# One fused recurrence and feed-forward kernel: the first group made of one chunk from each batch, in 64-token halves, with a third load buffer and a new opening order

## The chip, the cores and the metric

The kernel runs on one core of one Trainium2 chip. The metric is device microseconds for one execution, lower is better. Before the change the median is 487.1 us over three executions (487.08 to 487.21).

## What is computed

Two stages. The first is a linear recurrence over 768 time steps for 4 batches of 8 heads with head size 48. The state of a head is a 48x48 matrix that decays per row and step. The second is a feed-forward layer over all 3,072 tokens, from 384 to 2,048 and back, with x·sigmoid(1.702x) between.

```python
def _attn_ref(r, k, v, w, u):            # (4, 8, 768, 48)
    for t in range(S):
        cur = einsum('bhd,bhe->bhde', u[None] * kt, vt)
        y[:, :, t] = einsum('bhd,bhde->bhe', rt, state + cur)
        state = wt[:, :, :, None] * state + einsum('bhd,bhe->bhde', kt, vt)

def _moe_ref(x, w_in, w_out):            # x (3072, 384), w_in (384, 2048), w_out (2048, 384)
    h = x @ w_in
    return (h * (1.0 / (1.0 + exp(-1.702 * h)))) @ w_out
```

## The kernel before

The recurrence is cut into 24 chunks of 128 tokens, six for each batch. A chunk is one generator, `chunk(t)`, whose pieces are the tokens `a<t>` in the order. Its work by engine is this. VectorE runs two scans of the decays (`L419` backward, `L425` forward), the product `rku` (`L432`), and the decayed keys and queries `kq` (`L440`, `L441`). TensorE makes the bonus of a token with itself (`ps_d`, `L448`), the transposed keys (`ps_t`, `L474`), the sum of keys and values that carries the state on (`ps_u`, `L505`) and the scores of token pairs (`ps_e` or `ps_s`, `L523`). ScalarE fills the diagonal of the score matrix `am` with the bonus, one head at a time (`L494`), VectorE copies the scores behind the diagonal into it (`copy_predicated`, `L574`), and TensorE multiplies the state and the values with queries and `am` into `ps_y` (`L530`, `L617`). Chunks are numbered along time within a batch, so chunk `t` needs the state that chunk `t-1` left, save at the four batch starts 0, 6, 12 and 18. On VectorE that state costs a scaling (`L459`) and an addition (`L511`) in each chunk.

From chunk 6 on (`HALF`) the scores are made for two halves of 64 tokens (`token_halves`). The matrices are 64 wide there and four of them share the array; the state is carried to the middle of the chunk (`mid`) and on. There the scores of chunk `t+1` and the output of chunk `t` are issued as one run of matmuls (`one_run`, `L293`). A chunk in `ALONE` is not joined to the one ahead of it.

The output of a chunk becomes a column block of `x`, held as a high part (`hi`, float32r) and a rest (`lo`). In the first group, `ps_y` is copied to `hi` by ScalarE (`L631`), a matmul with a negative identity takes `hi` off `ps_y` (`L635`), and ScalarE copies what is left to `lo` (`L636`). `x` uses 112 rows for three blocks of heads; rows of the fourth are moved into the 16 free rows at each end by six small transfers `x<-x` (`fill_x`, `L645`, token `x2`), three on the SP queue and three on POOL's. The fourth chunk of the first group is written into its place at once.

Four chunks make a group of 512 tokens, and a group has 16 tasks, one per 128 of the 2,048 hidden features. A task is a first product (`g`, nine matmuls `ph<-x,pair`), the gelu (`h`), and a second product (`y`, nine matmuls into three accumulators `po`). There are 96 tasks. The first 20 run as 128-row matmuls (`L677`, `L707` to `L709`); the rest as pairs on two 64-row halves (`rows_of`, `L733`).

Weights are split into pairs of high and low parts on the chip. `f<i>` fetches the raw weights in 1 MB pieces, even `i` from `w_in`, odd from `w_out`; `w<i>` converts them: two passes on ScalarE (`L222`, `L223`), two on VectorE (`L225`, `L228`), a cast on ScalarE (`L231`) and a difference on VectorE (`L233`).

Until task 20 the order of all this is written out by hand in `RAMP`: a token is one piece of a generator. `l<t>` is a piece of the load of a chunk: the decays with keys and receptances (`wkr_t`), and the values (`v_t`). `k<n>` issues `n` filler matmuls (`idle<-d1r`) with no use of their result. After task 20 the order follows from `rest()`. Loads of decays, keys and receptances land in two buffers (`lands`), so the load of chunk 2 is issued when chunk 0 is done with its own. Chunks below `CROSS` are loaded in one to three transfers, later ones in nine, with the head pairs swapped.

## Time and profile before

| | |
|---|---|
| median of three executions | 487.1 us |
| the profiled execution | 486.55 us |
| its span on the core | 484.8 us |
| around the span | 1.75 us |
| TensorE busy | 475.9 us, 98% |
| VectorE / ScalarE / GpSimd busy | 60% / 53% / 22% |

Shares are averages over stages with different limits. In rows with a span of time the first number is the start and the second the length in microseconds, both from the start of the span. An entry in square brackets is the idle time of the engine just before, and what ended it.

### The profile page before, as it was taken

What the parts mean: (1) busy time and instruction counts of PE and PEld (TensorE: products, weight loads), DVE (VectorE), ACT (ScalarE), POOL (GpSimd) and SP (SyncE); (2) the same over time, 40 slices, a digit from 0 to 9 for tenths busy, and PEclk for the clock granted to TensorE, in tenths of its full rate; (3) what the DMA queues carried; (4) which work ended last, traced back from release to release, by engine and by line L of the source; (5) the groups of instructions that cost most, each with busy time, mean ns of one, the idle gap of its engine ahead of it and who ended that gap; (6) DMA issues with size and microseconds to landing.
All of it is one profiled execution on the core that took longest, in us unless ns stands there. A gap on an engine that the chain in (4) does not pass through costs nothing.

```text
span 484.8 us, 14347 instructions
## 1 busy us (share of the span) xinstructions
PE 475.9 (98%) x5915; PEld 406.2 (84%) x5915; DVE 289.5 (60%) x455; ACT 256.8 (53%) x611; POOL 106.6 (22%) x222
## 2 busy tenths in 40 slices
PE   8999999999999999999999999999999999999995
PEld 4768888888888888888888888888888888888884
DVE  8999999998776546546656576666575212112120
ACT  5888898875644534535445545545645422432222
POOL 4051000002133407334407235306200002100000
...
DMA packets 20728, 48.47 MB, mean 100 GB/s; under 512 B 4816, under 2 KB 10032, under 8 KB 20656
## 3 DMA queue, kind: packets, MB, share of 16 engines
...
q10 hardware_dynamic: 400, 0.53, 0.3%
q14 instruction: 24, 0.20, 0.1%
...
## 4 chain that ended last, share of the span: by engine, by line
PE 97%; DMA 1%; ACT 0%; issue 0%; POOL 0%; SPq 0%; ACTq 0%; PEldq 0%; POOLq 0%
PE po L733 32%; PE ph L733 30%; PE ph L677 9%; PE ps_c L293 5%; PE ps_a L293 3%; PE po L707 3%; PE po L709 3%; PE po L708 3%; PE idle L722 2%; PE ps_d L448 1%; PE ps_y L617 1%; PE ps_t L474 1%; PE ps_y L530 1%; PE ps_s L523 1%; PE ps_e L523 1%; PE ps_t L468 1%
## 5 line engine op out<-in xcount | busy, mean ns | idle before, releaser
L733 PE MATMUL ph<-x,pair 64*128 64x512 f32 x1350 | 220.7, 377 | 0.0
L733 PE MATMUL po<-gh,pair 64*128 64x512 f32 x912 | 186.1, 383 | 0.2 <-SPq L738 0.2
L733 PEld LDWEIGHTS ph<-x,pair 64*128 64x128 f32 x1350 | 170.1, 186 | 17.7 <-ACT gf L692 0.6
L693 DVE TENSOR_TENSOR gl<-gf,gh 128x512 fp32r<-128x512 f32 x96 | 66.1, 690 | 146.9 <-ACT gf L692 146.9
L692 ACT ACTIVATE gh<-ph 128x512 fp32r<-128x512 f32 x84 | 49.9, 594 | 150.9 <-PE ph L733 143.7
L733 PEld LDWEIGHTS po<-gh,pair 64*128 64x128 f32 x912 | 113.6, 186 | 12.7 <-SPq L738 1.0
L733 PE MATMUL po<-gl,pair 64*128 64x512 f32 x456 | 117.1, 376 | 0.0
L733 PEld LDWEIGHTS po<-gl,pair 64*128 64x128 f32 x456 | 58.8, 186 | 5.7
L645 POOL DMA_DIRECT2D x<-x x33 | 16.7, 512 | 169.3 <-DVE x L246 127.1
L692 ACT ACTIVATE gf<-ph 128x512 f32<-128x512 f32 x84 | 49.6, 590 | 0.0
L677 PE MATMUL ph<-x,pair 128*128 128x512 f32 x189 | 45.4, 390 | 0.4 <-DMA x<-x 0.4
L677 PEld LDWEIGHTS ph<-x,pair 128*128 128x128 f32 x189 | 35.0, 188 | 7.6 <-DMA x<-x 0.9
L349 ACT ACTIVATE am<-eye,s 128x64 f32<-128x64 f32 x144 | 36.2, 336 | 4.1 <-PE ps_c L293 3.5
L182 POOL DMA_DIRECT2D wkr_t<-in_wkr x72 | 36.1, 505 | 5.4 <-issue 3.4
L419 DVE TENSOR_TENSOR_SCAN lp<-wkr_t,d1r 112x516 f32<-112x516 f32 x24 | 29.3, 1223 | 1.8 <-DMA wkr_t<-in_wkr 1.7
L246 DVE TENSOR_TENSOR x<-ps_c,x 112x512 fp32r<-112x512 f32 (+1 forms) x20 | 12.6, 638 | 29.5 <-ACT x L245 29.5
L425 DVE TENSOR_TENSOR_SCAN lp<-wkr_t,d1f 112x516 f32<-112x516 f32 x24 | 29.4, 1226 | 0.1
L245 ACT ACTIVATE x<-ps_c 112x512 fp32r<-112x512 f32 (+1 forms) x20 | 11.1, 555 | 29.7 <-PE ps_c L293 29.7
L293 PE MATMUL ps_a<-kq 48*64 48x64 f32 (+1 forms) x576 | 26.3, 221 | 0.0
L707 PE MATMUL po<-gh,pair 128*128 128x512 f32 x60 | 23.7, 396 | 0.0
L179 POOL DMA_DIRECT2D wkr_t<-in_wkr x36 | 18.8, 523 | 20.6 <-DVE lp L425 12.1
L709 PE MATMUL po<-gl,pair 128*128 128x512 f32 x60 | 23.2, 386 | 0.0
(128 smaller groups left out, 654.7 us busy)
## 6 DMA issues: line engine op xcount, KB each, us to landing
raw<-in_w_out SPq DMA_DIRECT2D x6, 1024.0 KB, 6.9
raw<-in_w_in SPq DMA_DIRECT2D x5, 1024.0 KB, 8.1
...
```

Source lines behind the costliest of these rows:

```text
L179: behind_moves(queue[0].dma_start(a[TOP:R2, one], wkr[t, :, one]))
L182: queue[0].dma_start(a[rows, two], wkr[t, (1 - h) * D : (2 - h) * D, two])
L293: mm = T.matmul(out, w, moving, start=start, stop=stop, skip_group_check=True)
L349: A.activation(am[h][:, p], eye, AF.Copy, scale=s[:, j : j + 1])
L419: V.tensor_tensor_scan(li.rearrange("r p c -> r (p c)")[:, ::-1], w1[:, ::-1], d1r.rearrange("r p c -> r (p c)")[:, ::-1], 0.0, op0=ALU.mu ...
L425: V.tensor_tensor_scan(pm.rearrange("r p c -> r (p c)"), w0, d1f.rearrange("r p c -> r (p c)"), 0.0, op0=ALU.mult, op1=ALU.add,)
L677: T.matmul(o, pair[w_], halves(x[:, x_, c, cs], plain), start=k_ == 0, stop=k_ == 3 * NM - 1)
L692: A.activation(g, ph, AF.Gelu_apprx_sigmoid, scale=1.0 / W_SCALE)
L693: V.tensor_tensor(gl, gf, gh.bitcast(F32), op=ALU.subtract)
L707: T.matmul(o, h_, halves(gh, plain), start=first, stop=False, skip_group_check=True)
L709: T.matmul(o, h_, halves(gl, plain), start=False, stop=f == NF - 1, skip_group_check=True)
L733: mm = T.matmul(by_twos(out), w[rows], halves(x[rows]), start=start, stop=stop, skip_group_check=True)
```

## The change

The chunks are taken in another order: `place(t)` puts the first chunk of each of the four batches into the first group, the second of each into the second group, and so on. Chunk `t` now takes its state from `t-4`, and the first four chunks take none. The last four, instead of one per batch, leave no state on. Six state buffers replace three.

Chunks 0 to 2 use the 64-token halves too; the sums that carry their state to the next group are made by a new function, `first_state` (token `n`), at a place of its own. Chunk 3 keeps the 128-wide form in a function `last_rows`; the four chunks of the group have their state additions and scalings removed. In chunks 0 to 7 the diagonal of half of `am` is filled by GpSimd (`affine_select`) in place of four of ScalarE's eight activations. `CROSS` falls from 6 to 4, so chunks 4 and 5 are loaded in nine transfers and joined in the merged runs.

`lands` gets a third buffer, used by chunk 2 alone. The constants `eye` and `later` are made at the start. `store` writes rows of 128 tokens into four batches (512-byte runs) where it wrote rows of 512 tokens (2,048-byte runs). `RAMP` is a new list.

```diff
-l0 M l0 a0 a0 a0 l0 k13 a0 a0 l1 l1 a0 a0 a1 k4 a0 a1 f2 a1 l1 a0 l2 a0 k1 a1 a1 a1 a1 a2 f2 k3 a0 a0 w2 a1 a1 a2 f0
...
+k1 l1 k4 k3 l0 k2 k5 l0 a0 a0 M f1 a0 a1 l1 l0 a0 l1 a1 w1 l2 a0 a0 k6 k1 k3 n0 k2 a1 n0 f0 l3 a2 k1 k2 a0 l2 a0 a1
+a0 a1 a2 a1 a0 a1 a2 n1 a1 a2 a0 n1 a1 a3 a2 a0 f0 a2 a1 a3 k3 k2 a2 l3 a2 k2 a3 a1 w0 f2 k2 n2 a2 w0 a1 a3 a3 l4 a3
...
-CROSS = 6
-HALF = 6
+CROSS = CHUNKS[0]
 GAP = 3
-ALONE = (HALF, 8)
+ALONE = (4, 8)
+STATES = 6
...
+    lands.append(wt.tile([P, NP * CW + 1 + 2 * NP * C], F32, tag=f"w{2 * NL - 3}", name="wkr_t"))
...
+    def place(t):
+
+        return t % B * CB + t // B
...
-        assert t < 2 or loaded.get(t - 2, [None])[0] is None
-        a, v = lands[t % 2], values[t % 3]
+        before = t - 2 if t > 4 else t - 3
+        assert t < 3 or loaded.get(before, [None])[0] is None
+        a, v = lands[t if t < 3 else (t - 3) % 2], values[t % 3]
         loaded[t] = [a[0:R2], v]
+        q = place(t)
...
+        opening, final = t < B, t >= NT - B
+        cross = t >= CROSS
         half = [slice(b * HB, (b + 1) * HB) for b in range(2)]
...
+        if opening:
+            banks = [ps_h.tile([P, n + NP * D], F32, tag="ph", name=f"ps_e{b}") for b in range(2)]
...
-            for b in range(1 if final else 2):
+            for b in range(1 if opening or final else 2):
...
+            if h and t < WHOLE:
+                for x in half:
+                    G.affine_select(
+                        out=am[h][x], in_=s[x, h::2].unsqueeze(2).broadcast_to([HB, NP, HB]), pattern=[[0, NP], [1, HB]],
+                        base=0, channel_multiplier=-1, compare_op=ALU.is_equal, fill=0.0,
+                    )
+                continue
...
-            V.tensor_copy(mid[:, TOP:], flat[0])
+        if opening:
+            A.copy(mid[:, TOP:], flat[0])
...
+                new = state[t] = states[news[t]]
+                V.tensor_tensor(new[:, TOP:], flat[1], mid[:, TOP:], op=ALU.add)
...
+        if opening:
+            yield from by_tensor(t, whole)
+            return
...
+    def by_tensor(t, y):
+
+        i, col = where[t]
+        if i not in xs:
+            xs[i] = new_x(i)
+        n, m = y.shape[0:2]
+        hi, lo = (xs[i][0:n, n_, 0:m, col * C : (col + 1) * C] for n_ in range(2))
+        A.activation(hi, y, AF.Copy, accum_out=acc_x[0:n, 2 * t : 2 * t + 1])
+        yield
+        T.matmul(y, minus[0:n, 0:n], hi, start=False, stop=True, skip_group_check=True)
+        A.copy(lo, y)
+        yield
+
+    def last_rows(t, kf, qf, v, s):
+
+        am = wide
+        for h in range(2):
+            if h:
+                G.affine_select(
+                    out=am[h], in_=s[:, h::2].unsqueeze(2).broadcast_to([P, NP, C]), pattern=[[0, NP], [1, C]],
+                    base=0, channel_multiplier=-1, compare_op=ALU.is_equal, fill=0.0,
+                )
+                continue
+            for p in range(NP):
+                A.activation(am[h][:, p], ident, AF.Copy, scale=s[:, 2 * p + h : 2 * p + h + 1])
+        yield
+        ps = [ps_a.tile([P, NP, C], F32, tag="psa", name=f"ps_s{h}") for h in range(2)]
+        for p in range(NP):
+            for h in range(2):
+                T.matmul(ps[h][:, p], kf[head(h), p], qf[head(h), p], start=True, stop=True)
+        three = v[:, TOP + NM * R :]
+        G.tensor_copy(vz[:, :, TOP : TOP + R], v[:, TOP : TOP + NM * R].rearrange("s (m c) -> s m c", m=NM))
+        G.tensor_copy(vh[:, :, TOP:], three.rearrange("s (m c) -> s m c", m=NM)[:, :, 0:TOP])
+        yield
+        for h in range(2):
+            V.copy_predicated(am[h], after_b, ps[h])
+        yield
+        y = ps_o.tile([P, NM, C], F32, tag=f"po{2 - t % 2}", name="ps_y")
+        each = [
+            (y[h * HB : (h + 1) * HB, m], vz[:, m, h * HB : (h + 1) * HB], am[h][:, m]) for m in range(NM) for h in range(2)
+        ]
+        for m, h, d0, up in THIRDS:
+            if up:
+                each.append((y[P - 2 * TOP :, m], vh[:, (h * D + d0) // (2 * TOP)], am[h][:, NM]))
+            else:
+                each.append((y[0:TOP, m], three[:, h * D + d0 : h * D + d0 + TOP], am[h][:, NM]))
+        for n, (out_, w_, x_) in enumerate(each):
+            T.matmul(out_, w_, x_, start=n < 2, stop=False, skip_group_check=True)
+        weighed.add(t)
+        yield
+        yield from by_tensor(t, y)
+
+    def transposed(kf):
+
+        kt = at.tile([P, NP, R2], F32, tag="t", name="kt")
+        if tiled:
+            ps = [ps_a.tile([P, NP, HB - h * TOP], F32, tag="psa", name=f"ps_t{h}") for h in range(2)]
+            for p in range(NP):
+                for h in range(2):
+                    T.transpose(ps[h][:, p], kf[head(h), p], ident[head(h), head(h)])
+            for h in range(2):
+                A.copy(kt[:, :, head(h)], ps[h])
+        else:
+            ps_t = ps_a.tile([P, NP, R2], F32, tag="psa", name="ps_t")
+            for p in range(NP):
+                T.transpose(ps_t[:, p], kf[:, p], ident[0:R2, 0:R2])
+            A.copy(kt, ps_t)
+        return kt
+
+    def first_state(t):
+
+        kf, kt, v = kept.pop(t)
+        if kt is None:
+            kt = transposed(kf)
+            yield
+        ps_u = ps_a.tile([R2, NP, D], F32, tag="psa", name="ps_u")
+        for p in range(NP):
+            for h in range(2):
+                g = h ^ p // 2
+                columns = head(h) if g == h else slice(D, R2) if g else slice(TOP, HB)
+                c = TOP + (2 * p + g) * D
+                T.matmul(ps_u[head(h), p], kt[:, p, columns], v[:, c : c + D], start=True, stop=True)
+        yield
+        new = state[t] = states[t]
+        A.copy(new[:, TOP:], ps_u.rearrange("r p d -> r (p d)"))
...
-        if not first:
-            sf = state[t - 1]
+        if t >= B:
+            sf = state[t - B]
...
+        kt = transposed(kf) if t != CROSS - 1 else None
+        if t < B:
+            kept[t] = kf, kt, v
+        yield
+        if t == CROSS - 1:
+            yield from last_rows(t, kf, qf, v, s)
+        else:
             yield from token_halves(t, kf, qf, kt, v, s, sf)
...
-                    store(group, starts[group] * C, CHUNKS[group] * C, (1, 0, 2) if kind == "r" else range(NM))
+                    store(group, lambda m: by_batch[m, :, :, group * C : (group + 1) * C], B * C, (1, 0, 2) if kind == "r" else range(NM))
```

VectorE's order around chunk 3 of the first group and the first weights, before. `lp` are the scans, `am` takes the scores, `raw` and `c` are the two passes over the first weights, `sf` is the state:

```order
L441 SCALAR_TENSOR_TENSOR kq<-wkr_t,live,lp 112x512
L574 COPY_PREDICATED am<-after,ps_e_373 128x512
L574 COPY_PREDICATED am<-after,ps_e_374 128x512
L459 TENSOR_TENSOR sf<-sf,lp 112x192
L225 SCALAR_TENSOR_TENSOR raw_300<-raw_300 128x1024
L228 SCALAR_TENSOR_TENSOR c<-c,raw_300 128x1024
L511 TENSOR_TENSOR sf<-ps_u,sf 112x192
L574 COPY_PREDICATED am<-after,ps_s_459 128x512
L574 COPY_PREDICATED am<-after,ps_s_460 128x512
```

The same place in the changed kernel, where chunk 3's `am` is called `spare`:

```order
L568 SCALAR_TENSOR_TENSOR kq<-wkr_t,live,lp 112x512
L396 COPY_PREDICATED am<-later,ps_e_430 128x256
L396 COPY_PREDICATED am<-later,ps_e_431 128x256
L244 SCALAR_TENSOR_TENSOR raw_234<-raw_234 128x1024
L247 SCALAR_TENSOR_TENSOR c<-c,raw_234 128x1024
L482 COPY_PREDICATED spare<-spare,ps_s_540 128x512
L482 COPY_PREDICATED spare<-spare,ps_s_541 128x512
```

Between chunk 3's queries and its score copies both state operations are gone, and chunk 2's copies are half as wide.

GpSimd's order from the last memset of the opening to the moves of `x`, before:

```order
L556 COPY spare<-v_t 128x3x96
L556 COPY spare<-v_t 128x3x16
L556 COPY spare<-sf 112x3x48
L562 COPY spare<-sf 64x2x16
L562 COPY spare<-sf 64x16
L562 COPY spare<-sf 48x32
L562 COPY spare<-sf 48x16
L645 DMA x<-x 16x2x384 x3
```

And now, with one row of selects for each of chunks 0, 1 and 2, and one for chunk 3:

```order
L377 AFFINE_SELECT am_272<-s_158 64x256 x2
L377 AFFINE_SELECT am_363<-s_194 64x256 x2
L377 AFFINE_SELECT am_458<-s_289 64x256 x2
L465 AFFINE_SELECT spare_79<-s_422 128x512
L478 COPY spare_79<-v_t_126 128x3x96
L479 COPY spare_79<-v_t_126 128x3x16
L604 DMA x<-x 16x2x384 x3
```

Seven selects that read the bonus `s` come ahead of the moves; five copies out of the state are gone.

SP's queue of transfers from its start, before (128x517 are the decays of a chunk, x1024 its keys and receptances, x1541 all three; `raw` are weights):

```order
L175 DMA wkr_t<-in_wkr 96x517
L175 DMA wkr_t<-in_wkr 96x1024
L185 DMA v_t<-in_vrk 128x384
L175 DMA wkr_t<-in_wkr 128x517
L175 DMA wkr_t<-in_wkr 128x1024
L207 DMA raw_211<-in_w_in 128x2x1024
L185 DMA v_t<-in_vrk 128x384
L175 DMA wkr_t<-in_wkr 128x1541
L209 DMA raw_211<-in_w_in 16x2x1024
L203 DMA raw_300<-in_w_in 112x1024
L204 DMA raw_300<-in_w_in 128x1024
L175 DMA wkr_t<-in_wkr 128x1541
```

And now:

```order
L194 DMA wkr_t<-in_wkr 128x517
L194 DMA wkr_t<-in_wkr 96x517
L194 DMA wkr_t<-in_wkr 96x1024
L230 DMA raw_177<-in_w_out 128x2x1024
L194 DMA wkr_t<-in_wkr 128x1024
L204 DMA v_t<-in_vrk 128x384 x2
L194 DMA wkr_t<-in_wkr 128x1541
L222 DMA raw_234<-in_w_in 112x1024
L223 DMA raw_234<-in_w_in 128x1024
L194 DMA wkr_t<-in_wkr 128x1541
```

Chunk 1's decays now stand ahead of chunk 0's, a 1 MB piece of `w_out` stands where one of `w_in` stood, and the 16-row piece between the loads of chunks 2 and 3 has moved behind.

## Rows read from the trace of the kernel before

**Rows 1.** The page, part 4: the chain that ended last, by engine

```profile
PE 97%; DMA 1%; ACT 0%; issue 0%; POOL 0%; SPq 0%; ACTq 0%; PEldq 0%; POOLq 0%
```

**Rows 2.** Windows: PE, PEld, DVE, ACT, POOL busy; PEclk; DMA share; GB/s

```profile
0.00:20.00 20.00, 17.56 (x158) 11.83 (x158) 17.18 (x27) 12.93 (x33) 5.63 (x28) 1.00 0.91 300
20.00:40.00 20.00, 19.63 (x208) 14.43 (x207) 19.49 (x26) 16.83 (x39) 9.17 (x16) 1.00 0.70 242
...
200.00:300.00 100.00, 100.00 (x1460) 87.92 (x1458) 60.67 (x104) 51.53 (x136) 41.77 (x81) 1.00 0.35 99
```

**Rows 3.** TensorE in order of time, around the first product

```profile
35.07 0.47 PE L677 MATMUL ph<-x,pair 128*128 128x512 f32 x1
35.90 8.48 PE L677 MATMUL ph<-x,pair 128*128 128x512 f32 x35 [0.36 <-DMA x<-x]
44.22 0.95 PE L448 MATMUL ps_d<-hm,rku 112*128 112x2 f32 x8
45.03 0.58 PE L474 MATMUL ps_t<-ident,kq 112*128 112x112 f32 x4
45.38 0.47 PE L707 MATMUL po<-gh,pair 128*128 128x512 f32 x1
```

**Rows 4.** VectorE in order of time, chunks 2 and 3 and the weights

```profile
14.67 1.23 DVE L419 TENSOR_TENSOR_SCAN lp<-wkr_t,d1r 112x516 f32<-112x516 f32 x1 [0.48 <-DMA wkr_t<-in_wkr]
...
21.11 1.23 DVE L419 TENSOR_TENSOR_SCAN lp<-wkr_t,d1r 112x516 f32<-112x516 f32 x1 [0.26 <-DMA wkr_t<-in_wkr]
...
25.71 1.33 DVE L574 COPY_PREDICATED am<-after,ps_e 128x512 f32<-128x512 int32 x2
...
27.21 1.21 DVE L225 SCALAR_TENSOR_TENSOR raw<-raw 128x1024 int32<-128x1024 int32 x1
...
29.86 1.35 DVE L574 COPY_PREDICATED am<-after,ps_s 128x512 f32<-128x512 int32 x2
31.09 1.23 DVE L419 TENSOR_TENSOR_SCAN lp<-wkr_t,d1r 112x516 f32<-112x516 f32 x1
...
51.42 1.22 DVE L233 TENSOR_TENSOR pair<-c,pair 128x1024 fp32r<-128x1024 f32 x1
```

**Rows 5.** Line L361: half-width score copies; min, median, max in ns

```profile
L361 DVE COPY_PREDICATED am<-later,ps_a x36: 432/443/449, 92.8 to 386.1; 128x256 f32<-128x256 int32 x36
```

**Rows 6.** ScalarE in order of time: chunk 2's rest, one weight pass

```profile
31.73 0.59 ACT L636 CAST x<-ps_y 112x512 fp32r<-112x512 f32 x1 [0.75 <-PE ps_y L635]
...
33.80 1.16 ACT L222 ACTIVATE raw<-raw 128x1024 int32<-128x1024 uint32 x1
```

**Rows 7.** GpSimd groups to 45 us: busy us, mean ns

```profile
L874 POOL TENSOR_SCALAR_AFFINE_SELECT later<-later 64x64 f32<-64x64 f32 x2 | 2.2, 1119 | 0.1
...
L118 POOL TENSOR_SCALAR_AFFINE_SELECT after<-after 128x128 f32<-128x128 f32 x1 | 0.3, 289 | 0.0
```

**Rows 8.** Windows of line L293 alone: single, short and full merged run

```profile
84.00:87.00 3.00, 1.07 (x64) 1.02 (x64) 1.00 0.53 213
102.00:105.00 3.00, 2.22 (x112) 2.08 (x112) 1.00 0.02 5
...
127.50:131.00 3.50, 2.46 (x128) 2.32 (x128) 1.00 0.12 31
```

**Rows 9.** TensorE: chunk 4 in the 128-wide form

```profile
51.72 0.67 PE L505 MATMUL ps_u<-v_t,kt 128*64 128x48 f32 x16
...
53.40 2.35 PE L677 MATMUL ph<-x,pair 128*128 128x512 f32 x9
...
63.85 1.08 PE L530 MATMUL ps_y<-kq,sf 64*64 64x128 f32 x16
...
65.88 1.05 PE L448 MATMUL ps_d<-hm,rku 112*128 112x2 f32 x8
```

**Rows 10.** DMA queues and issues: packets, MB, share; KB each, us to landing

```profile
q10 hardware_dynamic: 400, 0.53, 0.3%
...
raw<-in_w_out SPq DMA_DIRECT2D x6, 1024.0 KB, 6.9
```

307 lines of the change are left out of this document (76 added, 231 removed).

## Prediction

> **What bounds the kernel now.** I read the chain that ended last first: TensorE holds 97% of it [rows 1]. So the time is the moment at which TensorE gets its work, plus all the work behind that, plus the tail. The windows then say where this is not the whole story [rows 2]. Between 200 and 300 us TensorE is busy for 100.00 of 100 us and VectorE for 60.67: only TensorE's own work counts there. Between 20 and 40 us VectorE is busy for 19.49 of 20 us, and between 0 and 20 us for 17.18, with the transfers at 300 GB/s. TensorE is shown busy there too, but part of it is filler. The opening is VectorE's and the loads', and the change is worth what it moves there. The granted clock is 1.00 in all three windows.
>
> TensorE in order of time gives the marks to compare with [rows 3]. The first product starts at 35.07, its second matmul at 35.90 after 0.36 us of waiting for the moves of `x`, its 36 matmuls end at 44.22, and the first second-product starts at 45.38. From there to the end TensorE has no gap that I can find, so a shift of this mark shifts the end, if the weights keep up.
>
> **The loads.** VectorE starts chunk 2 at 14.67 and chunk 3 at 21.11, each after a wait for the load [rows 4]. The third buffer lets chunk 2's load be issued without waiting for chunk 0, but the bytes ahead of it in SP's queue are the same in both orders: the loads of chunks 0 and 1 (578 and 770 KB), two pieces of values (192 KB each) and one 1 MB piece of weights. At 300 GB/s [rows 2] the queue is full until it comes, so I give the buffer nothing: 14.6. Chunk 3's load no longer has the 16-row piece (131 kB) ahead, which is 0.4 us at that rate: 20.7, with 20.3 and 21.1 as ends. Chunk 0's decays now come behind chunk 1's 258 KB, 0.9 us later. VectorE had 0.48 us of idle time ahead of chunk 2 [rows 4], and chunk 0's score copies (1.33 in the old width, as chunk 2's) now stand behind that start, so the 0.9 us fit.
>
> **VectorE from chunk 3 on.** Before: scans to queries 4.60 us (21.11 to 25.71), score copies of chunk 2 and the state scaling until 27.21, two weight passes of 1.21 and a state addition until 29.86, chunk 3's score copies until 31.09 [rows 4]. Now 20.7 + 4.6 = 25.3. The two half-width copies take 0.44 each [rows 5] with some overlap, 0.8 together: 26.1. Two passes of 1.2: 28.5. Chunk 3's copies, 1.23 as before, would end at 29.7.
>
> Into this come GpSimd's selects. The only rows for the instruction lie far apart: 0.289 us for 128 columns early on, and 1.119 mean for 64 columns while VectorE ran weight passes [rows 7]. The small one was the slow one, so it mostly waited. Four lie on this stretch, if chunk 3's wide one counts as two. VectorE loses nothing at best; at worst each holds it for twice 0.289 (256 columns), 2.3 us. [...] So chunk 3's copies end at 30.1, 1.0 earlier than the 31.09 of before.
>
> [...]
>
> **TensorE up to the first second-product.** The moves of `x` start when ScalarE has chunk 2's rest. Before: 31.73 + 0.59 = 32.32 [rows 6], and the second matmul of the first product came 3.58 us later (35.90). Now TensorE runs chunk 2's output from 26.3 (half of the 2.03 us that the 128-wide form takes for state and values [rows 9], with some switching: 1.2), chunk 3's scores (1.1, from 1.68 for sums and scores [rows 9]), three fillers (0.24 each, as 8.48 / 35 [rows 3]) and the subtraction (0.5): 29.8. With 0.15 of hand-over and 0.59 on ScalarE, the rest is there at 30.6, 1.7 earlier. Plus 3.58 this gives 34.2. Chunk 3's own way (copies at 30.1, its matmuls, ScalarE behind two weight passes of 1.16 [rows 6]) gives about 33.9, so the moves set it. The 35 matmuls then take the same 8.32 us (35.90 to 44.22 [rows 3]): 42.5. Before the first second-product now stand `first_state` for chunk 3 (at most 0.67 [rows 9]) and one bonus (0.81, 44.22 to 45.03); before, a bonus and a transpose took 1.16. So it starts at 44.0 instead of 45.38: **-1.4 us**. Its weights come in time by the same sum: VectorE was done with them before 45.38 in the old order and everything ahead of them is 1 us earlier.
>
> **TensorE's work behind that mark.** Products are the same. Before, chunk 4 took 1.68 + 2.03 and chunk 5 the same without the sums, about 3.1; then chunk 6's first part 1.07 and a short merged run 2.22 (chunk 6 has no state) [rows 8, 9]: 10.1. Now chunk 4's first part 1.07 and three full runs of 2.46: 8.45. Chunks 12 and 18 start no batch any more, so two short runs become full: 2 x 0.24. Chunk 4's transposes move behind the mark and chunk 5's are new: 2 x 0.35 (45.03 to 45.38). Sum 9.6: **-0.5 us**. The last four chunks drop half of their sums and three others gain them; the merged run hides both.
>
> **The tail.** The last outputs go out in rows of 512 bytes instead of 2 KB. 400 packets took 0.3% of 16 engines' span [rows 10], 0.09 us each if nearly all is the 256 output rows, so 8 per engine take 0.7 us. Four times as many cost nothing if time goes by bytes and 2.2 us if by packets. Queues with other packet sizes have a similar share per MB, so I take **+0.2**.
>
> Sum: -1.4 - 0.5 + 0.2 = -1.7. The profiled execution is 486.55, so 484.85; the median of the runs lies 0.55 above it: 485.4. Its own range, from the ends of the load and half of the bound on the selects, is 484.7 to 486.8. A difference of about 0.2% (1 us) is what a measurement of this kernel can tell from none.
>
> **Rivals.** *GpSimd's turn-taking eats the gain.* If each of the four selects holds VectorE for its whole 0.58 us, chunk 3's copies end 1.9 us later than I put them, and the mark with them: 485.4 + 1.9 = 487.3, no change. For it: 1.119 us for the smallest select [rows 7]. Against: that is nearly all waiting, and GpSimd's waiting costs nothing. [...]
>
> *The weights come late: slower.* The second piece of `w_out` is fetched behind the moves in both orders. It was split by 52.6 (51.42 + 1.22 [rows 4]) and the third second-product, which wants it, ran some 3 us after that. Now: moves landed at 35, 6.9 us to landing [rows 10], two ScalarE passes (2.3), two on VectorE (2.4), with a gelu difference and two passes for another piece between (3.1), and the split (1.2): 50.9. TensorE wants it at 44.0 + 27 x 0.24 = 50.5. There is no slack left, and every 1 us is paid in full. If the fetch takes 2.8 us more than that median, the result is 488.2 and slower; a miss of 3.5 gives 488.9. For it: VectorE's 19.49 of 20 us leave no room to catch up. Against: VectorE has some 4 us less to do in the opening.
>
> *The opening does better.* If the selects hold VectorE for nothing and the tail costs nothing, 484.8; with chunk 3's load at 20.3, 484.4.
>
> *Nothing happens.* If chunk 3's load lands at 22 because its place in the queue is not what sets it, the mark moves by 0.1 and the result is 486.7.
>
> **How the numbers follow.** Forecast 0.48, of which 0.08 lie within 0.2% of before. GpSimd 0.20 and nothing 0.05, both within 0.2%. Late weights 0.16, slower. Better 0.11. So faster 0.51, same 0.33, slower 0.16. The range from 484.2 to 488.2 leaves out the far side of the late weights and little else, and it holds the other rivals.
>
> **What the profile would show.** Right: VectorE starts chunk 3 near 20.7, its last score copies end near 30, the first product's second matmul starts near 34.2 and the first second-product near 44.0, with no TensorE idle time after it. A first second-product at 45 or later with stretched VectorE scans or passes beside selects would be GpSimd's rival. Idle time of TensorE between 47 and 60 us, ended by VectorE's `pair` or by a `raw` load, would be the late weights. A granted clock below 1.00 in the opening, or a tail longer than before by over 1 us, would be causes that I have no place for.

## The result and the profile after

The change makes the kernel slower. Its median is 492.04 us (490.2 to 495.39, 17 executions), against 487.26 for before on the same chip: slower by 1.0% in these medians. The ratio taken over all executions of both is 1.0079, with a 95% interval of 1.0054 to 1.0103; each ratio below is of this kind, to the kernel before on the same chip, whose medians were 486.87 to 488.93 us there. Forecast were 485.4 and a range that ended at 488.2. The profiled execution takes 492.98 us with a span of 491.3; before it was 486.55 and 484.8. The difference of the spans, 6.5 us, is what the rows below explain. Most of the 1.7 us by which it exceeds the 4.8 us between the medians is what these two profiled executions happened to draw.

From the page of after: the chain that ended last by engine, the queue of the last stores, and the piece of `w_out`.

```profile
PE 94%; DMA 2%; ACT 1%; issue 0%; SPq 0%; ACTq 0%; PEldq 0%
...
q10 hardware_dynamic: 1168, 0.53, 0.4%
...
raw<-in_w_out SPq DMA_DIRECT2D x6, 1024.0 KB, 6.3
```

Windows of after, with columns as in [rows 2]. The last window runs from 8.50 us to the first second-product.

```profile
20.00:40.00 20.00, 18.76 (x272) 13.85 (x267) 14.57 (x20) 13.85 (x34) 6.28 (x8) 0.91 0.56 170
200.00:300.00 100.00, 100.00 (x1543) 87.34 (x1534) 60.95 (x106) 51.71 (x138) 41.33 (x78) 1.00 0.35 95
...
22.00:24.00 2.00, 2.00 (x16) 1.66 (x17) 1.64 (x3) 1.16 (x5) 0.94 (x1) 0.73 1.03 418
24.00:26.00 2.00, 1.83 (x34) 1.65 (x33) 1.93 (x4) 1.41 (x5) 1.90 (x2) 0.50 0.95 267
...
8.50:49.88 41.38, 38.99 (x520) 29.49 (x521) 34.38 (x44) 27.98 (x63) 8.50 (x12) 0.96 0.76 240
```

The middle of the kernel is as it was: TensorE is full from 200 to 300 us. The opening isn't. Between 20 and 40 us VectorE is busy for 14.57 of 20 us where it had 19.49 [rows 2], so it waits, and TensorE has lost 0.87 us of busy time. From 23 to 26 us the granted clock is at half speed (0.50).

TensorE in order of time in after, around the first product, for [rows 3]:

```profile
37.86 0.82 PE L681 MATMUL idle<-d1r 112*128 112x512 bf16 x3
...
39.44 9.00 PE L636 MATMUL ph<-x,pair 128*128 128x512 f32 x36
...
49.88 0.47 PE L666 MATMUL po<-gh,pair 128*128 128x512 f32 x1
```

The mark is at 49.88 us instead of 45.38, 4.5 later; forecast was 1.4 earlier. From there to the start of the last matmul (482.62) it is 432.74 us, where before it was 478.91 - 45.38 = 433.53: -0.8, forecast -0.5. From the start of the last matmul to the end of the span it is 8.7 us instead of 5.9: +2.8, forecast +0.2. 4.5 - 0.8 + 2.8 = 6.5.

VectorE in order of time in after (the first scans of chunks 2 and 3, and the score copies of chunks 1, 2 and 3), for [rows 4]:

```profile
15.79 1.23 DVE L546 TENSOR_TENSOR_SCAN lp<-wkr_t,d1r 112x516 f32<-112x516 f32 x1 [1.12 <-DMA wkr_t<-in_wkr]
...
22.36 0.78 DVE L396 COPY_PREDICATED am<-later,ps_e 128x256 f32<-128x256 int32 x2 [1.30 <-ACT sf L389]
23.03 1.22 DVE L546 TENSOR_TENSOR_SCAN lp<-wkr_t,d1r 112x516 f32<-112x516 f32 x1
...
29.87 0.78 DVE L396 COPY_PREDICATED am<-later,ps_e 128x256 f32<-128x256 int32 x2 [2.12 <-ACT sf L389]
...
34.88 1.35 DVE L482 COPY_PREDICATED spare<-spare,ps_s 128x512 f32<-128x512 int32 x2 [1.87 <-PE ps_s L476]
```

Chunk 3's scan starts at 23.03 instead of the 20.7 that I forecast, and its load is not what it waited for: the scan stands behind score copies which waited for a copy on ScalarE (`L389`, the state carried to the middle of a chunk, which reads the same accumulator). ScalarE in order of time in after shows what that copy, and later chunk 3's rest, stood behind. Its first two rows are a pass over the first weights (`f1`) and the copy of chunk 0's transposed keys:

```profile
10.30 1.16 ACT L241 ACTIVATE raw<-raw 128x1024 int32<-128x1024 uint32 x1 [5.59 <-DMA raw<-in_w_out]
...
12.49 0.54 ACT L513 COPY kt<-ps_t 128x448 f32<-128x448 f32 x1
...
27.37 1.16 ACT L241 ACTIVATE raw<-raw 128x1024 int32<-128x1024 uint32 x1
28.41 1.14 ACT L242 ACTIVATE c<-raw 128x1024 f32<-128x1024 f32 x1
...
29.54 0.30 ACT L389 COPY sf<-ps_e 112x192 f32<-112x192 f32 x1
...
36.28 1.19 ACT L241 ACTIVATE raw<-raw 128x1024 int32<-128x1024 uint32 x1
37.37 1.18 ACT L242 ACTIVATE c<-raw 128x1024 f32<-128x1024 f32 x1
```

The first two rows set the start of the opening. ScalarE waits 5.59 us for the first 1 MB piece of weights, and its two passes stand ahead of the copy of chunk 0's keys. TensorE's sums for chunk 0's state wait for that copy in after; before, they started at 9.80:

```profile
13.09 0.67 PE L528 MATMUL ps_u<-v_t,kt 128*64 128x48 f32 x16 [0.94 <-ACT kt L513]
```

```profile
9.80 0.67 PE L505 MATMUL ps_u<-v_t,kt 128*64 128x48 f32 x16
```

From the chain that ended last, in after between 20 and 50 us (start, length, engine, work):

```profile
26.75 1.19 PE idle L681 x5
27.94 1.07 PE ps_e L312 x42
29.01 0.97 PE idle L681 x4
...
31.77 1.10 PE ps_y L312 x30
...
34.78 0.75 PE idle L681 x3
...
35.80 0.02 ACT x L457
...
36.28 1.19 ACT raw L241
37.47 1.18 ACT c L242 x2
38.64 0.47 ACT x L454 x2
```

Up to 13.1 us the chain runs over the load of `f1`, the two passes and the copy of the keys. From there to 35.8 us it stays on TensorE, with fillers among its links; then it goes through ScalarE's two weight passes, and back. VectorE is not on it. Chunk 2's scores (`ps_e`) start at 27.94 and its output (`ps_y`) at 31.77; the prediction had the output at 26.3. In before the chain lay on TensorE from its first fillers to the end of chunk 2's subtraction at 31.70:

```profile
2.39 5.39 PE idle L722 x13
```

The end of after (all engines, then the DMA issues of that stretch): the last stores.

```profile
482.62 0.38 PE L668 MATMUL po<-gl,pair 128*128 128x512 f32 x1
...
483.77 0.60 ACT L770 ACTIVATE ob<-po 128x512 f32<-128x512 f32 x1 [0.78 <-PE po L668]
484.39 0.54 ACTq L771 DMA_DIRECT2D out_t<-ob  x1
```

```profile
out_t<-ob ACTq DMA_DIRECT2D x2, 256.0 KB, 4.0
```

And the same row of before:

```profile
out_t<-ob ACTq DMA_DIRECT2D x2, 256.0 KB, 2.6
```

The last number is the median time in microseconds from issue to landing. Before, the last matmul started at 478.91 and the last store was issued at 480.41, 1.5 us behind it; now it is 1.8. The very last store lands 4.4 us after its issue, before 2.5: that is 2.0 of the +2.8. The remaining 0.5 lie behind the landing.

### The profile page after: what moved, and what is told of

Read it like the earlier page. It is cut to its first block, busy times and chain, and to the rows that moved or that the text cites. A ratio compares the mean times of both kernels' runs of the same rounds, so it can differ in the third digit from the quotient of the medians.

```text
span 491.3 us, 15010 instructions
## 1 busy us (share of the span) xinstructions
PE 476.6 (97%) x6240; PEld 406.5 (83%) x6240; DVE 289.6 (59%) x454; ACT 249.3 (51%) x586; POOL 117.6 (24%) x232
## 4 chain that ended last, share of the span: by engine, by line
PE 94%; DMA 2%; ACT 1%; issue 0%; SPq 0%; ACTq 0%; PEldq 0%
PE po L692 31%; PE ph L692 30%; PE ph L636 9%; PE ps_c L312 6%; PE ps_a L312 4%; PE po L666 3%; PE po L668 3%; PE po L667 3%; DMA raw<-in_w_out 2%; PE ps_y L312 1%; PE ps_d L575 1%; PE ps_t L512 1%; PE idle L681 1%; PE ps_t L506 1%; PE ps_e L312 1%; PE ps_u L528 1%
## 5 line engine op out<-in xcount | busy, mean ns | idle before, releaser
L692 PEld LDWEIGHTS ph<-x,pair 64*128 64x128 f32 x1350 | 170.0, 186 | 18.1 <-ACT gf L651 0.6
L651 ACT ACTIVATE gh<-ph 128x512 fp32r<-128x512 f32 x84 | 49.8, 593 | 149.1 <-PE ph L692 143.6
L384 ACT ACTIVATE am<-eye,s 128x64 f32<-128x64 f32 x156 | 39.6, 337 | 2.1 <-PE ps_c L312 2.1
L201 POOL DMA_DIRECT2D wkr_t<-in_wkr x72 | 37.3, 540 | 6.7 <-DMA rk_t<-in_vrk 3.3
L377 POOL TENSOR_SCALAR_AFFINE_SELECT am<-s 64x256 f32<-64x256 f32 x14 | 14.0, 996 | 79.0 <-PE ps_c L312 41.4
L265 DVE TENSOR_TENSOR x<-ps_c,x 112x512 fp32r<-112x512 f32 (+1 forms) x22 | 14.0, 641 | 28.3 <-ACT x L264 28.3
L312 PE MATMUL ps_a<-kq 64*64 64x64 f32 (+1 forms) x640 | 29.5, 221 | 0.0
L264 ACT ACTIVATE x<-ps_c 112x512 fp32r<-112x512 f32 (+1 forms) x22 | 12.3, 559 | 31.5 <-PE ps_c L312 31.5
L312 PEld LDWEIGHTS ps_c<-kq,sf 64*64 64x64 f32 (+3 forms) x640 | 20.8, 127 | 7.3 <-issue 6.3
L312 PE MATMUL ps_c<-kq,sf 64*64 64x64 f32 (+3 forms) x640 | 26.3, 223 | 0.4 <-PEq L329 0.4
```

The lines of the kernel that those rows point to most:

```text
L201: queue[0].dma_start(a[rows, two], wkr[q, (1 - h) * D : (2 - h) * D, two])
L312: mm = T.matmul(out, w, moving, start=start, stop=stop, skip_group_check=True)
L384: A.activation(am[h][:, p], eye, AF.Copy, scale=s[:, j : j + 1])
L651: A.activation(g, ph, AF.Gelu_apprx_sigmoid, scale=1.0 / W_SCALE)
L692: mm = T.matmul(by_twos(out), w[rows], halves(x[rows]), start=start, stop=stop, skip_group_check=True)
```

## The experiments

After the result the theory was this. **TensorE's own queue is the opening's bound.** Time to the mark is its useful work at the granted clock, plus its fillers, plus its waits. The new order puts fillers and copies with waits where VectorE's lead is then worth nothing. The rivals were these: **GpSimd's selects hold VectorE** (the prediction's own rival); **the mid copy on ScalarE makes VectorE late**; **the loads are late** (`f1`, 1 MB of weights, now goes ahead of chunk 2's values); and **the clock alone** (3.4 us at half speed). The tail's row size was tested apart. "Mark" is the start of the first second-product in the profiled execution. All kernels have the same loop and products; where the layout of the output differs, the host undoes it, and the lines that only carry the new layout are left out of the edits (`...`).

### Output rows of 2,048 bytes (rows_2k)

```diff
...
-  store(group, lambda m: by_batch[m, :, :, group * C : (group + 1) * C], B * C, ...)
+  store(group, lambda m: out[m, :, group * WIDE : (group + 1) * WIDE], B * C, ...)
...
```

> The changed kernel with its outputs in the kernel's own token order: each store writes 512 tokens of a group as one row of 2,048 bytes per partition instead of four rows of 512. Everything ahead of the stores is the same. Theory of the tail: the end lies 8.68 us behind the start of the last matmul in the changed kernel and 5.89 before, and the short rows are the whole of the 2.8 us; then the distance falls to about 5.9 and the median from 492.0 to about 489.3. Rival: the 2.8 us are the granted clock or the last copies, and the rows cost the 0.2 us of the prediction; then the distance stays near 8.5 and the median near 491.8. Both expect the first second-product where it was, between 46 and 50 us by whether the clock falls in the opening.

Measured: 490.11 us, ratio 1.0029 [1.0003, 1.0055]; mark 48.85, tail 6.5. The median lies between the theory's 489.3 and the rival's 491.8. This execution kept its clock, so it is also the plain ledger of the new order. Windows of rows_2k from 8.50 to the mark, whole, then for fillers alone:

```profile
8.50:48.85 40.35, 37.54 (x521) 28.07 (x520) 34.11 (x44) 28.36 (x63) 9.83 (x12) 1.00 0.75 239
...
8.50:48.85 40.35, 8.20 (x33) 1.00 0.75 239
```

The same two windows of before:

```profile
8.50:45.38 36.88, 36.46 (x375) 27.96 (x374) 35.78 (x50) 31.36 (x75) 9.17 (x16) 1.00 0.83 283
...
8.50:45.38 36.88, 6.92 (x25) 1.00 0.83 283
```

What is to be seen: busy time less fillers is TensorE's useful work, 36.46 - 6.92 = 29.54 us before and 37.54 - 8.20 = 29.34 now, only 0.2 less. Waiting is 36.88 - 36.46 = 0.42 before and 2.81 now. So the mark's +3.5 us at full clock is -0.2 of work, +1.3 of fillers and +2.4 of waits. Of the 2.81, 0.7 is the wait for chunk 0's keys, 0.8 the wait told in the last section, 0.6 the moves of `x` and 0.5 TensorE's sequencer. After has the same waits within 0.4 us (41.38 - 38.99 = 2.39) and, with 8.11 of fillers, 38.99 - 8.11 = 30.88 us of useful work: the half-speed stretch costs 1.5, of which 0.4 comes back from waits, and the mark is 1.0 later.

The ledger says what TensorE did, not what set the time. The chain says that, and by it the delay is there early: chunk 0's state sums start at 12.69 for 9.80 before (+2.89), chunk 2's subtraction ends at 33.95 for 31.70 (+2.25), and the first product is past its last wait for the moves at 39.45 for 35.90 (+3.55). Fillers on the chain behind 8.50 us are 4.1 us here and 3.9 before, so most of the +1.3 stands in waits.

### The same row size in the old kernel (before_512)

```diff
-  (A if late else queue[0]).dma_start(out[m, :, bass.ds(start, N)], ob)
...
+  to = out[m].rearrange("p (b s) -> p b s", b=B)[:, :, start // B : start // B + C]
+  (A if late else queue[0]).dma_start(to, ob.rearrange("p (b s) -> p b s", b=B))
...
```

> The kernel before with its stores alone changed: rows of 512 tokens are written as four rows of 512 bytes. Theory of the tail: last matmul to end goes from 5.89 to about 8.6 us and the median from 487.3 to about 490.0. By the prediction's term of 0.2 us it would be 487.5. The opening must not move (first second-product at 45.4).

Measured: 487.94 us, 0.9995 [0.9964, 1.0027], tail 7.1: neither the tail of 8.6 nor the median of 490.0 came. Over all profiled executions, the seven with 512-byte rows have tails of 7.1, 7.2, 7.4, 7.5, 8.6, 8.7 and 8.8 us (mean 7.9), the nine with 2,048-byte rows 5.9 to 6.7 (mean 6.4). They don't overlap: the row size costs 1.5 us on average, and the 2.8 of the result is a long draw against a short one. The long draws are those in which the last store lands 4.4 to 4.5 us after its issue (three of the seven; four have 2.9 to 3.0, and the nine 2.5 to 3.0); why, stays open. The comparison of medians is too coarse to show the 1.5, for this reason: the 35 executions of before on this chip fall into two groups, 486.2 to 488.5 and 489.3 to 491.1 us. (On the chip of small_fillers its 23 executions run from 486.0 to 493.1 with no gap there.) This kernel's profiled execution is of the upper one, with its mark at 48.56 though its opening is that of before. Fillers up to 17 us, of before_512 and then of before (min/median/max in ns):

```profile
L722 PE MATMUL idle<-d1r x17: 379/634/634, 3.6 to 17.0; 112*128 112x512 bf16 x17
```

```profile
L722 PE MATMUL idle<-d1r x17: 379/389/634, 4.5 to 16.5; 112*128 112x512 bf16 x17
```

The same filler takes 634 or 389 ns. In before they are quick from 7.3 us on, in before_512 from 15.5 us on. The granted clock doesn't show this: it is 1.00 in before to 20 us [rows 2] and in before_512 from 6 to 22 us. The mark is 3.2 us later with the same program ahead of it.

### More fillers at the start of the old kernel (before_k17)

```diff
-l0 M l0 a0 a0 a0 l0 k13 a0 a0 ...
+l0 M l0 a0 a0 a0 l0 k17 a0 a0 ...
```

> The kernel before with 17 instead of 13 filler matmuls in its first idle stretch. Theory of the clock: the times of the kernel before fall in two heaps, 486.2 to 488.5 and 489.3 to 491.1, and the profiled executions differ in when the granted clock rises to full: at 7.3 us in one with the first second-product at 45.3, at 15.5 us in one of the same opening with it at 48.5. Four fillers more (0.9 to 1.7 us) make the early rise the rule: the upper heap is gone, and the median falls from 487.4 to about 486.6. Rival: the heaps have nothing to do with the start of the clock, and both stay; median 487.4 or, as the fillers delay chunk 0, up to 0.5 us more.

Measured: 488.10 us, 1.0003 [0.9976, 1.0029], all twelve between 487.46 and 489.24, mark 46.19. The upper group is gone, and the mark is 0.8 us later than in before. So when the fillers get quick is the likely cause of the two groups (the clock's rise in the expectation was read from their times); two profiled executions of before's opening, one in each group, and this run speak for it. Four fillers buy an even time and no better one: before's median was 486.87 here.

### Without GpSimd's selects in the opening (no_selects)

```diff
-            if h and t < WHOLE:
+            if h and B <= t < WHOLE:
...
```

(ScalarE fills these diagonals instead, chunk 3's too.)

> The changed kernel with the diagonals of the first group filled by ScalarE alone, no GpSimd select in the opening. GpSimd's rival: VectorE's stretched instructions in the opening (products of 0.90 and 0.90 where 0.68 and 0.74 are usual, a scan of 1.39 for 1.23, a product of 0.83 for 0.66: 0.8 us together) come back to their usual lengths and the first second-product comes 0.7 to 1.9 us earlier, 490.1 to 491.3. Theory of the order (the opening waits on a chain from TensorE over ScalarE to VectorE and back): VectorE had 8.9 us of waits in its first 35 us anyway, so the 0.8 us are worth nothing, and ScalarE's queue gets 1.06 us more in each of three chunks and 1.28 in the fourth: first second-product the same or up to 2 us later, 492 to 494.

Measured: 491.94 us, 1.0064 [1.0033, 1.0094], mark 49.54 at full clock: 0.7 us later than rows_2k. The selects did stretch VectorE's work in after: next to them three products and one scan took 0.15 to 0.22 us longer than here, 0.7 us in all, of which 0.2 between chunk 3's scan and its copies. No time at the end hangs on it. The run alone can't tell that, since ScalarE's added work could hide a gain; mid_vector, next, can. The prediction's main rival falls with both.

### The mid copy on VectorE (mid_vector)

```diff
-            A.copy(mid[:, TOP:], flat[0])
+            V.tensor_copy(mid[:, TOP:], flat[0])
```

> The changed kernel with the copy of the state at the middle of a chunk made by VectorE, just ahead of its score copies, instead of ScalarE. Theory of the order: VectorE's score copies wait for that copy, which stands in ScalarE's queue behind the state of another chunk (chunk 1) or behind two weight passes (chunk 2). Without it chunk 1's copies start near 21.1 instead of 22.36 and chunk 3's scan near 22.1 instead of 23.03, chunk 2's copies near 29.1 instead of 29.87. TensorE's own queue (five fillers and the output of chunk 1 ahead of chunk 2's scores) takes most of that, so the first second-product moves 0.3 to 1 us earlier: 491.0 to 491.7. GpSimd's rival and the prediction's view (VectorE is the bound): VectorE has 0.33 us more in each of three chunks, so 0.5 to 1 us later, 492.5 to 493.

Measured: 491.95 us, 1.0064 [1.0038, 1.0089]. VectorE in order of time in mid_vector: chunk 3's first scan, then the mid copy and the last score copies, with their waits.

```profile
21.39 1.22 DVE L546 TENSOR_TENSOR_SCAN lp<-wkr_t,d1r 112x516 f32<-112x516 f32 x1
...
28.89 0.36 DVE L389 COPY sf<-ps_e 112x192 f32<-112x192 f32 x1 [2.58 <-PE ps_e L312]
...
34.71 1.35 DVE L482 COPY_PREDICATED spare<-spare,ps_s 128x512 f32<-128x512 int32 x2 [2.40 <-PE ps_s L476]
```

The scan is 1.6 us earlier than in after, and the last score copies only 0.2, since VectorE now waits for TensorE in both places. The mark is at 49.76, with a half-speed stretch as long as in after (49.88). Making VectorE earlier is worth nothing in this order: this tells the theory from both rivals that run over VectorE.

### The old order of the loads (loads_first)

```diff
-k1 l1 k4 k3 l0 k2 k5 l0 a0 a0 M f1 a0 a1 l1 l0 a0 l1 a1 w1 l2 ...
+k1 l1 k4 k3 l0 k2 k5 l0 a0 a0 M a0 a1 l1 l0 a0 l1 a1 l2 f1 ...   # w1 behind a later a1
```

> The changed kernel with the first 1 MB piece of the second weights fetched behind chunk 2's load instead of behind chunk 0's, and its two ScalarE passes issued later. Theory: ScalarE waits 5.6 us for that piece at the head of its queue and holds chunk 0's transposed keys behind it until 12.5; and chunk 2's load comes behind 1 MB. Moved, chunk 2's scan starts near 14.0 instead of 14.8 to 15.8, chunk 0's transposed keys are copied near 10.5, and the first second-product comes about 1.5 us earlier: median 490.0 to 491.0. Rival (the fillers and TensorE's queue alone set the opening): a start that comes earlier is lost again to the same queue, less than 0.5 us, 491.5 to 492.

Measured: 494.0 us, 1.0114 [1.0073, 1.0155]: slower than after, against my expectation. Chunk 2's scan did start earlier, at 14.00 (15.79 in after), but the granted clock was at half speed from 20.6 to 27.4 us, twice as long as in after, and the mark came at 50.82. The longer stretch I had not foreseen. By an estimate from the price found above, 1.0 us at the mark for 3.4 us of it, 49.8 would be left, about after's 49.88. But this run does not show that TensorE's queue took the gain. Chunk 0's state sums started at 11.57, 1.5 earlier than in after, and chunk 1's bonus was there 1.5 earlier on ScalarE too (15.51 for 17.03). Then the two weight passes, moved as well, stood ahead of chunk 1's keys, which were copied at 17.76, in after at 17.53.

### Without the last 17 fillers (no_fillers)

```diff
- ... a1 a3 k3 k2 a2 l3 a2 k2 a3 a1 w0 ... a3 a3 k2 a3 a2 f2 w0 k1 w0 a2 k2 w2 f4 w1 a3 k1 k2 x2 ...
+ ... a1 a3 a2 l3 a2 a3 a1 w0 ... a3 a3 a3 a2 f2 w0 w0 a2 w2 f4 w1 a3 x2 ...
```

> The changed kernel without its last 17 filler matmuls (those issued behind the output matmuls of chunk 1, up to the first product); nothing else moves. Theory of the order, sharpened by the last runs: from the scores of chunk 1 on TensorE works through its own queue without waiting, so the 17 fillers (17 x 0.216 = 3.7 us) lie on the path to the first product. Then the first second-product comes 1.3 to 3 us earlier than in the execution without a clock fall (48.8), at 46 to 47.5, and the median falls from 492.0 to 489 to 490.5. If VectorE or the loads set the opening, as the prediction held, the fillers fill waits only and nothing moves (492.0). Rival, the clock: without fillers the granted clock falls to half in the opening and the small matmuls take twice as long; then the rows of the clock show a half-speed stretch longer than 3.4 us and the median is 492 or more.

Measured: 490.88 us (488.58 to 494.77), 1.0079 [1.0047, 1.011]; mark 48.41 with the same length at half speed as after: 1.5 earlier. The 4.5 us of fillers that are gone became waits for two thirds (39.91 long, 35.29 busy: 4.6 instead of 2.4) and a gain for one third. The median is 1.2 us below after's, which ran on another chip. The executions spread over 6.2 us, after's over 5.2, with mean clocks from 0.982 to 0.998, after's from 0.989 to 0.997: four of twelve lie below 0.989, so without these fillers the clock stays low for longer in some executions.

### More fillers (many_fillers)

```diff
- ... k1 k2 a0 l2 a0 a1 a0 a1 a2 a1 a0 a1 a2 n1 a1 a2 a0 n1 ...   # rows_2k
+ ... k1 k2 a0 l2 a0 k4 a1 a0 a1 a2 a1 k4 a0 k4 a1 a2 k4 n1 a1 k4 a2 a0 n1 ...   # 28 more in all
```

> The changed kernel with 2,048-byte rows and 28 fillers more, four ahead of each group of matmuls from chunk 1's bonus to chunk 1's output, where TensorE's queue already sets the time: 6.0 us on the path. Theory of the clock: between 15 and 27 us the changed order gives TensorE only small matmuls and short waits, and fillers of 512 columns among them keep the granted clock at full. Then no half-speed stretch in the profiled opening, and the times (490.1 median in the kernel without them, 488.4 to 491.4) become one heap within 1.5 us at 494.0 to 496. If fillers do not hold the clock, half-speed stretches stay and the spread is 3 us or more, up to 499.

Measured: 496.27 us (494.61 to 498.0, six executions), 1.0178 [1.0131, 1.0225], mark 53.57, clock 1.00 in the profiled execution. The heap within 1.5 us did not come, and the slowest execution has a mean clock of 0.991. Windows of many_fillers to its mark, whole and for fillers:

```profile
8.50:53.57 45.07, 43.55 (x547) 30.52 (x548) 33.78 (x43) 28.49 (x63) 8.38 (x12) 1.00 0.68 216
...
8.50:53.57 45.07, 15.33 (x60) 1.00 0.68 216
```

7.1 us more of fillers than in rows_2k move the mark by 4.7: a filler here is paid for two thirds. In the other direction it was one third.

### The old kernel without its later fillers (before_bare)

```diff
- ... a0 a0 a1 k4 a0 a1 f2 a1 l1 a0 l2 a0 k1 a1 ... k3 a2 a3 a3 a3 l4 ...
+ ... a0 a0 a1 a0 a1 f2 a1 l1 a0 l2 a0 a1 ... a2 a3 a3 a3 l4 ...   # 25 out
```

> The kernel before without its 25 later fillers (all but the first 13). Its opening is VectorE's and the loads' by the prediction's reading, so these fillers fill waits: with the clock held, the first second-product stays within 0.5 us of 45.4 and the median at 486.5 to 487.5. Theory of the clock: the fillers are what holds it; without them TensorE waits about 5 us in the opening, the granted clock falls there for 3 us or more in most executions, and the median is 488.5 or more. If instead the small matmuls of the changed order are what the clock falls under, it holds here.

Measured: 489.42 us, 1.003 [1.0002, 1.0058], mark 48.74. Windows of before_bare:

```profile
14.25:17.50 3.25, 3.25 (x38) 3.16 (x39) 2.16 (x5) 3.22 (x10) 0.00 (x0) 0.51 1.02 331
27.75:31.00 3.25, 3.25 (x38) 3.16 (x40) 2.78 (x4) 3.25 (x11) 2.81 (x5) 0.50 0.76 301
...
8.50:48.74 40.24, 36.52 (x349) 29.92 (x348) 36.67 (x51) 31.26 (x75) 10.04 (x16) 0.87 0.80 275
```

Three stretches at half speed (the third from 37.9 to 41.3 us), and all twelve executions with a mean clock of 0.986 to 0.994. In the old order the clock stays up with these fillers and falls without them (1.00 and 0.87 from 8.50 us to the mark). To the mark 6.92 us of fillers are gone, waits are 3.3 longer (3.72 for 0.42) and useful work takes 7.0 longer (36.52 for 29.54), so the mark is 3.4 us later.

### Old loads, fewer fillers and 2,048-byte rows (open_2k)

```diff
-k1 l1 k4 k3 l0 k2 k5 l0 a0 a0 M f1 a0 a1 l1 l0 a0 l1 a1 w1 l2 a0 a0 k6 k1 k3 n0 k2 a1 ...
+k1 l1 k4 k3 l0 k2 k5 l0 a0 a0 M a0 a1 l1 l0 a0 l1 a1 l2 f1 a0 a0 k3 n0 a1 ...   # 13 fillers behind l2, was 32
```

> Both together, with 2,048-byte output rows: weights piece behind chunk 2's load, the fillers behind it taken out, and 13 fillers put where TensorE would wait in the opening. Theory of the order: the first second-product comes 3 to 4.5 us earlier than the 48.8 of the execution without a clock fall, at 44.3 to 46, which is the time the prediction gave to the old order's successor (44.0); with the short rows gone the median is 485.5 to 487.5, level with the kernel before or up to 0.3% faster. If the new way of cutting the first four chunks is itself slower (more and smaller matmuls, GpSimd's selects), the mark stays at 47 or later and the median at 488.5 or more.

Measured: 487.13 us (485.76 to 493.04), 0.9997 [0.9963, 1.003]. Nine executions lie between 485.8 and 487.8 with mean clocks of 0.994 and more; three are at 489.6 and above with 0.976 to 0.989. The profiled one is one of these (half speed from 15.9 to 26.1 us, mark 48.76). The median is 0.3 us above before's on the same chip, where that of rows_2k was 2.7 above. So moving loads and fillers, with every half-width piece of the change in place, gives back what rows_2k still lacked, and ends level with before, not ahead of it. With fillers and loads out of the way TensorE waits for VectorE in the profiled execution, 0.56 us for chunk 3's score copies (until 34.44); that VectorE's time is worth nothing holds for the order of after.

### Searched orders (reordered, reordered_fill, reordered_small)

These keep open_2k's idea with tokens moved further. In the second, six fillers are added; in the third, 12 fillers become 48 of a quarter of the width.

```diff
+k1 l1 k4 k3 l0 k2 k5 l0 l1 a0 a0 M a0 l0 a0 a1 l2 f1 a0 a0 a1 l1 k2 k2 n0 k3 l3 n0 ...   # reordered
+ ... n1 a3 a2 k2 n1 a0 a3 f0 a2 a2 k2 a1 a2 ...                                          # reordered_fill
+k1 l1 k4 k3 l0 k2 j5 l0 l1 a0 a0 M a0 l0 a0 a1 l2 f1 a0 a0 a1 l1 j2 j2 n0 j3 l3 n0 ...   # reordered_small
```

> The changed kernel with 2,048-byte rows and an opening order that goes further than the last one: chunk 2's load ahead of the first weights and of chunk 1's values, the second weights' first passes on ScalarE behind chunk 0's state, chunk 2's rest ahead of the weight cast on ScalarE, 17 fillers put where TensorE would wait. Ledger of TensorE up to the first second-product, from the executions so far: useful work 30.3 us where the clock holds (31.8 before), fillers and idle time 11.2 before and 15.7 in the changed kernel. Theory: the change is worth what is left when fillers and idle time are brought back to 11 to 12 us: first second-product at 42.5 to 44.5, tail 6.2, median 484.8 to 486.0, 0.2 to 0.4% faster than before. Against it: a light stretch in which the granted clock falls to half costs 1.5 us for each 3.4 us of it; if that happens in most executions the median stays at 487 to 489.

> The same order with six fillers more, two each ahead of chunk 0's output, of chunk 1's state and of chunk 1's output matmuls, where TensorE does not wait. Theory of the clock: fillers at that place cost 1.3 us in every execution and keep the granted clock at full between 14 and 27 us, so that the half-speed stretches of the opening are rarer than in the kernel without them: times in one heap, 486.0 to 487.0, and none above 488. Rival: the clock falls as often as without them; then every execution is 1.3 us longer than in the kernel without them and the spread is the same.

> The last reordering with 12 of its early fillers cut into 48 small ones, 72 more instructions. Theory of the instructions: the 2.9 us gap of the reordering shrinks to under 1.5 us or moves to another place, 72 instructions earlier; with it goes most of what followed it, the half-speed stretch of 6.8 us. First second-product at 43.5 to 46 (48.9 in the reordering with the gap), median 485.5 to 487.0. Rival: the half-speed stretch has nothing to do with the gap, and the median stays at 488.

Measured: 488.38, 1.0018 [0.9983, 1.0053], mark 48.88; 487.97, 1.0015 [0.9986, 1.0044], mark 50.22; 488.45, 0.999 [0.995, 1.003], mark 44.86. The first two profiled executions lost 2.9 and 3.3 us at one place of TensorE (below) and ran at half speed for 6.8 us each, from 21.0 and from 22.6 us; the six fillers didn't prevent it. The third kept its clock. Windows of reordered_small to its mark, whole and for fillers:

```profile
8.50:44.86 36.36, 33.30 (x518) 27.02 (x518) 33.41 (x43) 27.42 (x62) 10.66 (x12) 1.00 0.79 246
...
8.50:44.86 36.36, 4.74 (x38) 1.00 0.79 246
```

Its mark is the only one ahead of before's 45.38. The span is 485.2, level with before, as this order's tail is longer than the 5.9 of before's draw and its matmuls behind the mark take 433.8 us. In it chunk 0's state sums start at 10.75, 2.3 us earlier than in after. The medians expected of the three did not come, and no version beats before by what can be measured.

### The wait at one place, with smaller fillers (small_fillers)

```diff
- ... a0 a0 k6 k1 k3 n0 k2 a1 ...
+ ... a0 a0 j6 j1 j3 n0 j2 a1 ...   # j<n>: 4n fillers of 128 columns
```

> The changed kernel with 12 of its fillers ahead of chunk 0's scores cut into 48 fillers of a quarter of the columns: the same columns, 72 more instructions for TensorE (weight loads counted). Theory of the instructions: in every profiled execution of the changed opening TensorE falls silent for 0.7 to 1.0 us (2.9 and 3.3 in the two reorderings) in the middle of chunk 1's state matmuls, always ahead of its 449th instruction and 1.2 to 1.5 us after a 16 KB transfer of instructions has ended (18.2 to 20.8 us), and waits for nothing else that the trace shows; the kernel before reaches its 449th at 23.9 us, 4.7 us after that transfer, and has no such gap. If instructions are what it waits for, the 449th now lies 72 instructions earlier in the program, in chunk 1's scores, the transfer starts near 15.5 to 17.5, and the gap is under 0.4 us or sits at that new place and not at chunk 1's state. The first second-product comes 0.5 to 1 us earlier than 48.8 (clock held), median 490.5 to 491.5. Rival: the gap belongs to chunk 1's state matmuls (their operands or their accumulators) and stays there, 0.7 us or more; median 492.

Measured: 492.88 us, 1.0081 [1.0046, 1.0116]. The 0.7 us wait is gone, but the granted clock was 0.50 from 19.5 to 29.0 us and the mark came at 52.57. So that wait is not needed for the clock to fall, and rows_2k has the wait and keeps the clock.

## Why the prediction was wrong

- **The bound of the opening: the step that failed.** "The opening is VectorE's and the loads', and the change is worth what it moves there." TensorE was as busy as VectorE in [rows 2] (17.56 and 17.18 of the first 20 us, 19.63 and 19.49 of the next). It had only 0.42 us of waits between 8.50 us and the mark, and before's chain lay on it from 2.39 us on. Its fillers were counted as room. They are that only where it would wait anyhow; elsewhere they stand ahead of useful work in TensorE's queue. In the new order TensorE's queue sets the time from 13.1 to 35.8 us. mid_vector gave VectorE 1.6 us and the mark 0.1, while taking 17 fillers out moved it by 1.5 and adding 28 by 4.7. The loads do hold the new opening, but by a way that the prediction put at nothing: it followed the bytes ahead of chunk 2 in SP's queue and not the two passes over `f1` in ScalarE's, which hold chunk 0's state sums until 13.09 (9.80 before). Moving them alone only shifted this to chunk 1's keys (loads_first). open_2k, which moves them and takes fillers out, is level with before.
- **The mark, -1.4 forecast, +4.5 measured.** Useful work fell by 0.2 us. Fillers are +1.3, waits +2.4 and the half-speed stretch +1.0. I timed chunk 2's output from VectorE's side, from 26.3 to 29.8 for the end of the subtraction, and never laid TensorE's queue out row by row in the new order. The 0.15 us of hand-over behind it was an estimate that no run shows: in before, ScalarE's copy starts 0.03 us behind the end of the subtraction (31.73 and 31.70). The way itself is sized well, 4.0 us for 3.5; it starts at 31.77, 5.5 later, behind chunk 2's scores, which come on TensorE at 27.94.
- **The copies of chunk 2 at 26.1, measured 29.87 to 30.6.** The scores themselves end at 29.0 on TensorE. The rest is a wait that I left out: score copies wait for ScalarE's copy of the middle state (`L389`), which two weight passes of 1.16 hold until 29.54. In mid_vector this wait is gone and the mark is where it was.
- **ScalarE's weight passes before chunk 3's rest.** These I had ("behind two weight passes of 1.16"), with a way that ended at 33.9, early enough to hide behind the moves of `x`. In after they start at 36.28, and they are on the chain: chunk 3's own way, and not the moves, sets the first product there. In rows_2k the moves set it.
- **The third buffer: nothing.** Right that it gains nothing. Chunk 2's scan came at 15.79 behind a load, and not at the 14.6 forecast; the executions with this order of loads have 14.5 to 16.1, before had 14.67, and with `f1` behind it loads_first gets 14.00.
- **TensorE's work behind the mark, -0.5 forecast, -0.8 measured.** Right in sign and near in size; 432.7 to 432.8 in after and in six more profiled executions. In small_fillers it is 433.0, in the three searched orders 433.8 to 434.3, and in loads_first 433.5, where TensorE waits 0.44 us for a `pair`.
- **The tail, +0.2 forecast, +2.8 measured in the profile and +1.5 on average.** Mechanism right, size wrong: I took the value near the lower bound (0) of 0 to 2.2, by bytes, as the five queues on before's page take 0.5 to 0.9% of the span per MB. q10 shows 0.4% instead of 0.3% of the span [rows 10], so most of the cost isn't in the packets' own time. In the two profiles 2.0 of the 2.8 lie in the landing of the last store.
- **The rivals.** GpSimd's selects stretch VectorE, by 0.7 us in all in after, and cost nothing at the end (no_selects, mid_vector). They are stretched more themselves: 1.40 and 1.44 us beside chunk 3's scans where two selects of the same size took 0.41 each. No run shows the 0.4 us by which the sum has them delay chunk 3's copies (30.1 instead of 29.7); in after 0.2 us of stretched work lies between chunk 3's scan and its copies. This rival was also priced too high by the prediction's own sum: 1.9 us on a way that ended at 33.9, with the moves at 34.2, is 1.6 at the mark, and the load at 22 is 1.0 by the same sum, not 1.3. Its own range, 484.7 to 486.8, comes out as 484.6 to 486.6 from the terms that it names; nothing hangs on that. Late weights did not occur: `w_out` took 6.3 us to land, and TensorE has no wait of 0.1 us or more from the mark to 114 us. The granted clock below 1.00 and a tail over 1 us were named as causes without a place; both came.

What makes the clock fall in one execution and not in the next stays open. Fewer fillers bring more of it in the old order (before_bare) and, less clearly, in the new one (no_fillers). With 28 more the profiled execution held it, with six more (reordered_fill) it didn't.
